# Head of a fused attention and MLP kernel: two raw weight loads behind the stores, sums of squares accumulated on ScalarE, three weight pairs by 16-bit instructions, four filling groups for six

## The chip, the cores and the metric

The kernel runs on one core of one Trainium2 chip. The metric is device time in microseconds (us), the median of several runs. The engines are TensorE (PE in the profile; PEld are its weight loads), VectorE (DVE), ScalarE (ACT), GpSimd (POOL) and SyncE (SP, which issues all transfers of this kernel). Sixteen DMA engines move the data.

## The reference

Three stages follow each other on 2176 tokens of width 512 (4 batches, 8 heads of width 64):

```python
# attention: 32 global tokens see everything; 512 local tokens see the global ones and a band of +-32
s_ll = np.where(np.abs(pos[:, None] - pos[None, :]) <= 32, scale * q_l @ k_l.T, -1e9)
out_l = softmax([scale * q_l @ k_g.T, s_ll]) @ [v_g, v_l]
out_g = softmax(scale * q_g @ [k_g, k_l].T) @ [v_g, v_l]
x = [out_g, out_l] as (B * S, H * D)
# first MLP
xn = x / np.sqrt(np.mean(x * x, axis=-1, keepdims=True) + 1e-06) * rms_g
x = (silu(xn @ w_gate) * (xn @ w_val)) @ w_out          # 512 -> 1536 -> 512
# second MLP
r = np.maximum(x @ w_in, 0.0)
return (s * (r * r) + b) @ w_out2                       # 512 -> 2048 -> 512
```

All inputs are float32.

## The kernel before

**Groups.** The tokens are worked on in five groups of at most 512. The first group is the 512 local tokens of batch 0. For each group come the first MLP (12 slices of its inner width) and the second MLP (16 slices). Between the matmuls of a group, the attention of the next group's tokens is strewn in small steps.

**Weights.** The weights come as 34 pairs of blocks, in the order in which PE uses them. Each block is 512 x 128, and each product is made of three matmuls (L691 to L693) with a high and a low part of both operands: 24 matmuls a pair. A pair arrives as raw 64-bit numbers (1 MB, `load_raw`, tile `wr`, four buffers). `conv_begin` takes the raw numbers apart: ScalarE multiplies the upper 32-bit word into tile `cv` (L192), VectorE makes the missing bits in tile `ce`, clamps `cv` (L205) and joins both (L206). The missing bits are made in one of two ways: with `halves`, two 16-bit instructions on VectorE (L197, L199); without, a copy on ScalarE (L202) and one VectorE instruction (L203). `conv_end` casts the high part on ScalarE (L213), takes the low part on VectorE (L214), loads the next raw pair, and stores the finished pair to device memory (tile `wsc`, 1 MB, L217). Only the first group converts; the others load the stored pairs.

**The head** (`start`). Before the first matmul with weights, the attention of batch 0 must be done, in four units of two heads. Unit u goes through `S_` (scores on PE, then on VectorE the mask, the maximum and the difference, L313 to L315, called a score block in this document, then the exponential on ScalarE, L320), `T_` (transposes on PE, L623, two copies on ScalarE, L624) and `V_` (values on PE, L329, then the shares on VectorE, L336 to L338, then the squares on ScalarE, L634 or L637). `first_norm` makes the inverse root from the sums of squares, scales the four column blocks of the tokens (L538, L540), transposes them on PE (L547) and writes the high and low parts of x (L552, L553). `fill` issues matmuls whose results are not used (L600); one stands ahead of the transposes of `first_norm`.

**Order.** PE's order in the head is written out by `in_turn`, the order of ScalarE, VectorE and SP by `in_line`, which puts each instruction of a list behind the one before it. Pairs 0 and 1 are converted inside the head with `halves`; pair 2 is begun there without `halves` and ended behind the first Silu (`ending`). Behind that, `conv` converts pair n + 4 when PE is through with pair n, and a scheduler fills in the order that the lists leave open. The engines take their instructions strictly in order. SP issues a transfer when the eighth one before it has landed and the buffer is free.

## Time and profile before

| | |
|---|---|
| median of 3 runs | 931.55 us (931.52 to 933.0) |
| the profiled execution | 932.3 us, its span 930.5 us |
| PE busy | 910.2 us, 98% of the span |
| ScalarE, VectorE busy | 389.5 us (42%), 435.4 us (47%) |
| mean granted TensorE clock | 0.989 |
| moved by DMA | 255.77 MB, mean 275 GB/s |
| first matmul of the main part | 43.62 us from the start of the span |

The span runs from the first to the last instruction. A share of busy time is a mean over the head, the first group (in which all weights are converted) and the four others. What a change in one stage is worth is read in that stage.

### The profile page before, as it was taken

How to read it: one execution, taken by the hardware profiler on the slowest of the kernel's cores; microseconds unless marked ns; L12 is line 12 of the kernel's file. 1: busy time of each engine (PE TensorE's matmuls, PEld its weight loads, DVE VectorE, ACT ScalarE, POOL GpSimd, SP SyncE). 2: the span in 40 equal slices, each digit the busy share in tenths (PEclk: the TensorE clock that was granted, in tenths of full speed). 3: DMA queues.
4: the chain of work that ended last, by engine and by line, in shares of the span. 5: the costliest groups of instructions: out<-in, count | busy, mean ns of one | idle time of the engine just before them, and what ended most of it. 6: DMA issues, size and time to landing. Idle time of an engine off the chain costs nothing.

```text
span 930.5 us, 16330 instructions
## 1 busy us (share of the span) xinstructions
PE 910.2 (98%) x6946; PEld 776.0 (83%) x6946; DVE 435.4 (47%) x754; ACT 389.5 (42%) x558; POOL 0.6 (0%) x7
## 2 busy tenths in 40 slices
PE   9799999999999989999999999999999999999998
PEld 6477887877887868888878868888899999999998
DVE  5898889979642232343242232344222244321333
ACT  2787997969433132233223132232233133211322
POOL 0000000000000000000000000000000000000000
PEclk7899999999999999999999999999999999999999
DMA  9999999997976664755566654654588887798780
GB/s 365 392 379 425 368 425 423 395 347 293 372 262 229 246 259 142 276 188 181 205 229 242 241 205 141 211 185 177 197 317 299 287 282 269 281 341 306 286 300 29
DMA packets 43960, 255.77 MB, mean 275 GB/s; under 512 B 5104, under 2 KB 9456, under 8 KB 15984
## 3 DMA queue, kind: packets, MB, share of 16 engines
q1 hardware_dynamic: 43888, 254.73, 73.1%
q8 instruction: 55, 0.90, 0.4%
q14 instruction: 17, 0.14, 0.0%
HBM read 214.60 MB, written 40.11 MB: 274 GB/s over the span
## 4 chain that ended last, share of the span: by engine, by line
PE 94%; ACT 2%; DVE 1%; issue 1%; DMA 1%; SPq 0%; ACTq 0%
PE m L691 16%; PE m L692 16%; PE m L693 16%; PE acc L692 12%; PE acc L691 12%; PE acc L693 12%; PE at L329 2%; PE at L289 1%; PE acc L600 1%; PE at L324 1%; PE at L374 1%; PE at L406 1%; DMA s_k<-in_k_dram 1%; PE at L486 1%; PE m L623 1%
## 5 line engine op out<-in xcount | busy, mean ns | idle before, releaser
L692 PE MATMUL acc<-h,wt 128*128 128x512 f32 (+1 forms) x536 | 193.2, 360 | 0.6 <-DVE h L799 0.3
L693 PE MATMUL acc<-h,wt 128*128 128x512 f32 (+1 forms) x536 | 192.1, 358 | 0.0
L691 PE MATMUL acc<-h,wt 128*128 128x512 f32 (+1 forms) x536 | 185.2, 362 | 0.4 <-ACT h L153 0.4
L691 PE MATMUL m<-x,wt 128*128 128x512 f32 (+1 forms) x480 | 173.0, 361 | 1.9 <-ACT sg L766 1.9
L692 PE MATMUL m<-x,wt 128*128 128x512 f32 (+1 forms) x480 | 172.3, 359 | 0.0
L693 PE MATMUL m<-x,wt 128*128 128x512 f32 (+1 forms) x480 | 172.2, 359 | 0.0
L776 DVE TENSOR_TENSOR a<-sg,m 128x512 f32<-128x512 f32 (+1 forms) x60 | 36.4, 607 | 174.5 <-PE m L693 166.2
L691 PE MATMUL m<-y,wt 128*128 128x512 f32 (+1 forms) x320 | 115.2, 360 | 2.8 <-DVE t L796 2.8
L692 PE MATMUL m<-y,wt 128*128 128x512 f32 (+1 forms) x320 | 115.4, 361 | 0.3 <-DVE y L728 0.3
L693 PE MATMUL m<-y,wt 128*128 128x512 f32 (+1 forms) x320 | 114.8, 359 | 0.0
L796 DVE SCALAR_TENSOR_TENSOR t<-m,ct,r 128x512 f32<-128x512 f32 (+1 forms) x80 | 53.6, 670 | 129.7 <-ACT r L795 129.3
L692 PEld LDWEIGHTS acc<-h,wt 128*128 128x128 f32 x536 | 100.6, 188 | 14.4 <-DVE h L799 1.9
L691 PEld LDWEIGHTS acc<-h,wt 128*128 128x128 f32 x536 | 100.4, 188 | 14.4 <-ACT h L153 0.8
L693 PEld LDWEIGHTS acc<-h,wt 128*128 128x128 f32 x536 | 100.7, 188 | 12.5 <-issue 0.2
L795 ACT ACTIVATE r<-m 128x512 f32<-128x512 f32 (+1 forms) x80 | 42.4, 533 | 156.5 <-PE m L693 156.1
L691 PEld LDWEIGHTS m<-x,wt 128*128 128x128 f32 x480 | 90.0, 188 | 14.7 <-ACT sg L766 2.8
L692 PEld LDWEIGHTS m<-x,wt 128*128 128x128 f32 x480 | 90.1, 188 | 11.5 <-DVE x L553 0.2
L693 PEld LDWEIGHTS m<-x,wt 128*128 128x128 f32 x480 | 90.1, 188 | 11.3
L766 ACT ACTIVATE sg<-m 128x512 f32<-128x512 f32 (+1 forms) x60 | 32.0, 534 | 129.3 <-PE m L693 129.2
L799 DVE SCALAR_TENSOR_TENSOR h<-t,ct,h 128x512 fp32r<-128x512 f32 (+1 forms) x79 | 53.1, 672 | 40.2 <-ACT h L798 36.8
L798 ACT ACTIVATE h<-t,ct 128x512 fp32r<-128x512 f32 (+1 forms) x79 | 52.3, 662 | 44.7 <-DVE t L796 39.9
L691 PEld LDWEIGHTS m<-y,wt 128*128 128x128 f32 x320 | 60.4, 189 | 11.0 <-DVE t L796 3.3
(158 smaller groups left out, 953.3 us busy)
## 6 DMA issues: line engine op xcount, KB each, us to landing
wt<-wsc SPq DMA_DIRECT2D x136, 1024.0 KB, 4.9
wr<-in_w_dram SPq DMA_DIRECT2D x34, 1024.0 KB, 9.1
wsc<-wt SPq DMA_DIRECT2D x34, 1024.0 KB, 8.6
vr<-in_v_dram SPq DMA_DIRECT2D x12, 1105.0 KB, 8.5
fk<-in_k_dram SPq DMA_DIRECT2D x12, 784.0 KB, 6.2
fq<-in_q_dram SPq DMA_DIRECT2D x12, 272.0 KB, 7.8
out_dram<-z SPq DMA_DIRECT2D x12, 256.0 KB, 4.2
s_v<-in_v_dram SPq DMA_DIRECT2D x2, 1040.0 KB, 8.9
```

Source lines behind the costliest of these rows:

```text
L289: mms.append(PE.matmul(bk[32 * g:32 * g + 32, h, 128 * c:128 * c + 128].rearrange("p (a n) -> p a n", a=2), lhsT=qr[x, SG + 32 * i:SG + 32 ...
L324: in_turn([PE.transpose(flat[:, 128 * a:128 * a + 128], pp[:, a], ident) for a in range(8)])
L329: return [PE.matmul(bk[32 * g:32 * g + 32, h, 65 * c:65 * c + 65], lhsT=t(4 * h + c, g), rhs=vr(4 * c + g)[:, 65 * h:65 * h + 65]) for c i ...
L691: mms = [PE.matmul(out_, lhsT=wh, rhs=xh, start=first, stop=False), PE.matmul(out_, lhsT=wh, rhs=xl, start=False, stop=False), PE.matmul(o ...
L692: PE.matmul(out_, lhsT=wh, rhs=xl, start=False, stop=False),
L693: PE.matmul(out_, lhsT=wl, rhs=xh, start=False, stop=last)]
L766: recent["A"] = A.activation(out=sg[:, :N], in_=gb[:, :N], func=AF.Silu)
L776: V.tensor_tensor(out=a[:, :N], in0=sg[:, :N], in1=vb[:, :N], op=ALU.mult)
L795: A.activation(out=r[:, :N], in_=hb[:, :N], func=AF.Relu)
L796: V.scalar_tensor_tensor(out=t[:, :N], in0=hb[:, :N], scalar=ct[:, C_S:C_S + 1], in1=r[:, :N], op0=ALU.mult, op1=ALU.mult)
L798: recent["A"] = A.activation(out=h[:, 0, :N], in_=t[:, :N], func=AF.Identity, bias=ct[:, C_B:C_B + 1])
L799: recent["V"] = V.scalar_tensor_tensor(out=h[:, 1, :N], in0=t[:, :N], scalar=ct[:, C_B:C_B + 1], in1=h[:, 0, :N].bitcast(F32), op0=ALU.add ...
```

## The change

The first batch of raw loads is three instead of four; the first of them is issued ahead of the second unit's values, the second ahead of the fourth's. The fourth raw load stands behind the store of pair 0 on SP's queue, the fifth behind the store of pair 1, and the loads of the first attention units, which stood behind the fourth raw load, stand behind the fifth. The sums of squares of units 2 and 3 are accumulated on ScalarE in four instructions each, as those of units 0 and 1 were; before, one instruction squared the whole and VectorE summed. The fourth column block is scaled on VectorE. Pair 2 is converted with `halves`, wholly behind the first Silu, and one more raw load is issued behind it. The filling ahead of the norm's transposes has four matmuls for six. The lists of ScalarE and VectorE in the head are written anew. The first attention step of the first group is let off 12 us after the group's start by the planner's count, not 10.

```diff
@@ conv_end @@
-        nc.sync.dma_start(out=wsc[n], in_=wn.bitcast(F32))
+        stores[n] = nc.sync.dma_start(out=wsc[n], in_=wn.bitcast(F32))
@@ load_qk @@
-                in_line([raws[3], d])
+                in_line([raws[4], d])
@@ first_norm @@
-            if c == 3:
-                scaled.append(A.mul(out=o, in_=o, mul=r[:, c:c + 1]))
-            else:
-                scaled.append(V.tensor_scalar(out=o, in0=o, scalar1=r[:, c:c + 1], scalar2=None, op0=ALU.mult))
+            scaled.append(V.tensor_scalar(out=o, in0=o, scalar1=r[:, c:c + 1], scalar2=None, op0=ALU.mult))
@@ start @@
         ld_qk(3)
+        load_raw()
         ld_v(1)
         ld_v(2)
         load_raw()
         ld_v(3)
-        for _ in range(3):
-            load_raw()
+        load_raw()
...
-            if u < 2:
-                sq[u] = [A.activation(out=j[:, c], in_=uu[:, c], func=AF.Square, accum_out=ss[:, c, u:u + 1])
-                         for c in range(4)]
-            else:
-                sq[u] = A.activation(out=j, in_=uu, func=AF.Square)
-                rd[u] = V.tensor_reduce(out=ss[:, :, u], in_=j, axis=mybir.AxisListType.X, op=ALU.add)
+            sq[u] = [A.activation(out=j[:, c], in_=uu[:, c], func=AF.Square, accum_out=ss[:, c, u:u + 1])
+                     for c in range(4)]
...
-            roots, r, scaled, xa, xd = first_norm(sm, lambda b: fill(b, 6))
+            roots, r, scaled, xa, xd = first_norm(sm, lambda b: fill(b, 4))
...
-        g2, a2, d2 = conv_begin(2)
-        in_line([ex[0], ex[1]] + cp[0] + [ex[2]] + cp[1] + [ex[3]] + cp[2] + sq[0] + [a0[0]] + cp[3] + sq[1]
-                + [a1[0], a0e, sq[2], a2[0], sq[3], a1e] + roots + [scaled[3]] + xa + [a2[1]])
-        in_line([am[0], am[1], am[2], am[3], ev[0], d0[0], d0[1], d0[2], d0[3], ev[1], d1[0], d1[1], ev[2], d1[2], d1[3], ev[3],
-                 rd[2], rd[3], sums, r[0], r[1]] + scaled[:3] + [d0e] + xd + [d1e, d2[0], d2[1], d2[2]])
-        begun.append(d2[2])
-        ending.append(lambda: conv_end(2, g2))
+        in_line([stores[0], raws[3]])
+        in_line([stores[1], raws[4]])
+        in_line([ex[0], ex[1], a0[0]] + cp[0] + [ex[2]] + cp[1] + [a1[0], ex[3]] + cp[2] + [a0e] + sq[0] + cp[3]
+                + sq[1] + sq[2] + sq[3] + roots + xa + [a1e])
+        in_line([am[0], am[1], d0[0], d0[1], am[2], d0[2], am[3], d0[3], ev[0], d1[0], d0e, ev[1], d1[1], ev[2], ev[3],
+                 d1[2], sums, r[0], r[1]] + scaled + [d1[3]] + xd + [d1e])
+        begun.append(d1e)
+
+        def third_pair(sg):
+            g2, a2, d2 = conv_begin(2, True)
+            in_line([a1e, sg, a2[0]])
+            in_line([d1e, d2[0], d2[1], d2[2], d2[3]])
+            conv_end(2, g2)
+            load_raw()
+
+        ending.append(third_pair)
@@ main loop @@
-            sched["ok"] = sched["t"] + (0.0 if gi else 10.0)
+            sched["ok"] = sched["t"] + (0.0 if gi else 12.0)
...
-                in_line([recent["A"], ending.pop(0)()[0]])
+                ending.pop(0)(recent["A"])
                 conv(C_LEAD - 1)
```

The order on three queues, first before, then of the change. SP's queue in the head, from its 11th transfer on (`wr` are raw loads, `s_v`, `s_w` and `s_r` values of the units 1 to 3, `wsc0` and `wsc1` the stores of pairs 0 and 1, `fq` and `fk` the loads of the first attention units):

```order
L576 DMA s_v_112<-in_v_dram 128x2080
L576 DMA s_w_116<-in_v_dram 128x1950
L576 DMA s_r_115<-in_v_dram 128x130
L171 DMA wr_132<-in_w_dram 128x1024
L576 DMA s_w_117<-in_v_dram 128x1950
L576 DMA s_r_115<-in_v_dram 128x130
L171 DMA wr_136<-in_w_dram 128x1024
L171 DMA wr_138<-in_w_dram 128x1024
L171 DMA wr_140<-in_w_dram 128x1024
L265 DMA fq_744<-in_q_dram 128x544
L265 DMA fk_745<-in_k_dram 128x1568
```

Of the change:

```order
L171 DMA wr_129<-in_w_dram 128x1024
L573 DMA s_v_112<-in_v_dram 128x2080
L573 DMA s_w_116<-in_v_dram 128x1950
L573 DMA s_r_115<-in_v_dram 128x130
L171 DMA wr_134<-in_w_dram 128x1024
L573 DMA s_w_117<-in_v_dram 128x1950
L573 DMA s_r_115<-in_v_dram 128x130
L171 DMA wr_138<-in_w_dram 128x1024
L217 DMA wsc0_625<-wt_620 128x2048
L171 DMA wr_623<-in_w_dram 128x1024
L217 DMA wsc1_639<-wt_634 128x2048
L171 DMA wr_637<-in_w_dram 128x1024
```

The first raw load moved from place 14 to 11, the second from 17 to 15, the third stands where it stood, and behind it nothing is issued before the store of pair 0.

VectorE in the head, from the third score block on (`s_p_150` and `s_p_148` are its results, `ce_613` and `cv_614` belong to pair 0, `ce_627` to pair 1):

```order
L313 TENSOR_TENSOR acc1_248<-acc1_248,ct_102 128x16x32
L314 TENSOR_REDUCE mx_290<-acc1_248 128x8
L315 TENSOR_TENSOR s_p_150<-acc1_248,mx_290 128x1024
L313 TENSOR_TENSOR acc0_308<-acc0_308,ct_102 128x16x32
L314 TENSOR_REDUCE mx_349<-acc0_308 128x8
L315 TENSOR_TENSOR pm0_105<-acc0_308,mx_349 128x1024
L336 TENSOR_SCALAR rs_400<-at_367 128x8
L337 RECIPROCAL rs_400<-rs_400 128x8
L338 TENSOR_TENSOR u_152<-at_367,rs_400 128x2x4x64
L197 TENSOR_SCALAR ce_613<-wr_132 128x1024
L199 TENSOR_SCALAR ce_613<-wr_132 128x1024
L205 TENSOR_SCALAR cv_614<-cv_614 128x1024
```

Of the change:

```order
L197 TENSOR_SCALAR ce_613<-wr_129 128x1024
L199 TENSOR_SCALAR ce_613<-wr_129 128x1024
L313 TENSOR_TENSOR acc1_246<-acc1_246,ct_102 128x16x32
L314 TENSOR_REDUCE mx_288<-acc1_246 128x8
L315 TENSOR_TENSOR s_p_148<-acc1_246,mx_288 128x1024
L205 TENSOR_SCALAR cv_614<-cv_614 128x1024
L313 TENSOR_TENSOR acc0_306<-acc0_306,ct_102 128x16x32
L314 TENSOR_REDUCE mx_347<-acc0_306 128x8
L315 TENSOR_TENSOR pm0_105<-acc0_306,mx_347 128x1024
L206 SCALAR_TENSOR_TENSOR cv_614<-cv_614,ce_613 128x1024
L336 TENSOR_SCALAR rs_398<-at_365 128x8
L337 RECIPROCAL rs_398<-rs_398 128x8
```

The conversion of pair 0 moved from behind the first shares to between the second and the fourth score block.

VectorE late in the first group, in the second MLP (`at_2153` and `at_2155` are the values of an attention unit that PE computes in a burst, `m_2258` and `m_2260` the product of one inner slice; L796, in the change L798, frees that bank):

```order
L336 TENSOR_SCALAR rs_2210<-at_2153 128x8
L206 SCALAR_TENSOR_TENSOR cv_2275<-cv_2275,ce_2274 128x1024
L337 RECIPROCAL rs_2210<-rs_2210 128x8
L338 TENSOR_TENSOR u_1262<-at_2153,rs_2210 128x2x4x64
L414 TENSOR_SCALAR rg_2214<-at_2153 128x1
L796 SCALAR_TENSOR_TENSOR t_2289<-m_2258,ct_102,r_2288 128x512
L415 RECIPROCAL rg_2214<-rg_2214 128x1
L214 TENSOR_TENSOR wt_2281<-cv_2275,wt_2281 128x2x512
L416 TENSOR_SCALAR og_1451<-at_2153,rg_2214 128x64
L796 SCALAR_TENSOR_TENSOR t_2337<-m_2307,ct_102,r_2336 128x512
```

Of the change, without the five rows ahead (L336, L337, L338, L203, L414), up to the next L798:

```order
L798 SCALAR_TENSOR_TENSOR t_2291<-m_2260,ct_102,r_2290 128x512
L205 TENSOR_SCALAR cv_2228<-cv_2228 128x1024
L415 RECIPROCAL rg_2216<-rg_2216 128x1
L206 SCALAR_TENSOR_TENSOR cv_2228<-cv_2228,ce_2227 128x1024
L416 TENSOR_SCALAR og_1462<-at_2155,rg_2216 128x64
L203 TENSOR_SCALAR ce_2276<-ce_2276 128x1024
L205 TENSOR_SCALAR cv_2277<-cv_2277 128x1024
L206 SCALAR_TENSOR_TENSOR cv_2277<-cv_2277,ce_2276 128x1024
L801 SCALAR_TENSOR_TENSOR h2_2292<-t_2291,ct_102,h2_2292 128x512
L214 TENSOR_TENSOR wt_2234<-cv_2228,wt_2234 128x2x512
L798 SCALAR_TENSOR_TENSOR t_2339<-m_2309,ct_102,r_2338 128x512
```

Nine instructions, six of them of conversions, stand between the two, where there were three. On PE the burst of values moved too: before, it stood three matmuls ahead of the end of `m_2307`, whose successor needs the bank of `m_2258`; now 22 matmuls (12 of an output slice, 10 of `m_2309`) stand between the burst and the successor.

## Rows read from the trace of the kernel before

**Rows 1.** The page, part 4: the chain that ended last, shares of the span.
```profile
PE 94%; ACT 2%; DVE 1%; issue 1%; DMA 1%; SPq 0%; ACTq 0%
```
**Rows 2.** Waits of PE, whole kernel: us in total, times, longest.
```profile
PE m L691 <- DVE t L796: 2.8, 2, 2.1
```
**Rows 3.** Timeline of PE, 26 to 44: start, us, what, count, idle before.
```profile
27.32 0.30 PE L329 MATMUL acc<-s_v,ptf 128*32 128x65 f32 x3 [2.61 <-issue]
...
33.50 0.27 PE L329 MATMUL at<-s_w,ptf 128*32 128x65 f32 x1 [3.00 <-issue]
...
34.08 8.03 PE L600 MATMUL acc<-ones 128*128 128x512 f32 x12
...
40.23 1.02 PE L600 MATMUL acc<-ones 128*128 128x512 f32 x2
...
41.95 1.91 PE L547 MATMUL acc<-ct,u 128*128 128x128 f32 x16
...
43.62 0.71 PE L691 MATMUL m<-x,wt 128*128 128x512 f32 x2
```
**Rows 4.** Instruction queue: whole kernel, 31.0:31.5, 280.4:280.5 (packets, MB, share); engines at 280.
```profile
q8 instruction: 55, 0.90, 0.4%
...
q8 instruction: 1, 0.02, 13.3%
...
q8 instruction: 1, 0.02, 72.1%
...
280.00:281.00 1.00, 1.00 (x6) 0.47 (x6) 0.23 (x1) 0.73 (x2) 0.00 (x0) 1.00 0.45 172
```
**Rows 5.** SP's 11th transfer: its issue, and its time from issue to landing.
```profile
6.60 0.33 SPq L576 DMA_DIRECT2D s_v<-in_v_dram  x1
...
s_v<-in_v_dram SPq DMA_DIRECT2D x1, 1040.0 KB, 9.8
```
**Rows 6.** Timeline of VectorE, 16 to 43.
```profile
16.57 0.70 DVE L313 TENSOR_TENSOR acc<-acc,ct 128x512 f32<-128x512 f32 x1 [2.10 <-PE acc L305]
...
18.56 1.23 DVE L315 TENSOR_TENSOR s_p<-acc,mx 128x1024 f32<-128x1024 f32 x1
...
24.85 0.74 DVE L197 TENSOR_SCALAR ce<-wr 128x1024 int16<-128x1024 int16 x1
...
35.39 0.16 DVE L336 TENSOR_SCALAR rs<-at 128x8 f32<-128x8 f32 x1
...
36.43 0.68 DVE L638 TENSOR_REDUCE ss<-s_j 128x4 f32<-128x512 f32 x1
...
38.03 0.17 DVE L657 TENSOR_REDUCE ss<-ss 128x4 f32<-128x16 f32 x1
...
39.45 1.28 DVE L540 TENSOR_SCALAR u<-u,r 128x512 f32<-128x512 f32 x3
```
**Rows 7.** Timeline of ScalarE, 25 to 50.
```profile
25.84 0.32 ACT L634 ACTIVATE s_j<-u 128x128 f32<-128x128 f32 x1
...
27.02 1.13 ACT L192 ACTIVATE cv<-wr 128x1024 f32<-128x1024 f32 x1
...
28.31 1.07 ACT L624 COPY ptf<-m 128x512 f32<-128x512 f32 x2 [0.17 <-PE m L623]
...
33.39 1.03 ACT L213 CAST wt<-cv 128x1024 fp32r<-128x1024 f32 x1
...
49.46 1.89 ACT L202 COPY ce<-wr 128x2048 int16<-128x2048 int16 x1
```
**Rows 8.** VectorE at 207; engines, 210 to 220 (sums, PEclk, DMA share, GB/s).
```profile
207.08 0.17 DVE L336 TENSOR_SCALAR rs<-at 128x8 f32<-128x8 f32 x1 [1.52 <-PE at L406]
...
210.00:220.00 10.00, 10.00 (x37) 8.14 (x38) 8.34 (x14) 9.97 (x15) 0.00 (x0) 0.83 0.99 388
```
**Rows 9.** Engines in two stretches of the first group (PE, PEld, DVE, ACT, POOL, PEclk, DMA).
```profile
60.00:70.00 10.00, 10.00 (x104) 8.00 (x103) 9.95 (x13) 10.00 (x10) 0.00 (x0) 1.00 1.01 421
...
230.00:240.00 10.00, 10.00 (x46) 8.29 (x45) 8.71 (x16) 5.24 (x9) 0.00 (x0) 1.00 0.61 216
```

More of the change, by code (lines that the diff above doesn't have):

```diff
@@ L141, in attn_moe_kernel @@
     wt, wraw, wsc, left = {}, {}, {}, {}
-    raws = {}
+    raws, stores = {}, {}
     nraw = [0]
```

## The prediction, made before the kernel ran

> **What bounds the kernel now.** I read the chain that ended last first: TensorE (PE) holds 94% of it [rows 1]. So time can only be won where PE waits, or where it does work that is not part of the result. I then read PE's waits over the whole kernel and its timeline in the first 45 us. PE reaches the first matmul of the main part (L691) at 43.62 us, and from there on it hardly waits. The largest later wait for one engine is 2.8 us in two pieces, for VectorE's L796 [rows 2]. The head is different: two waits, 2.61 and 3.00 us, end in "issue", which means that nothing in the profile ends them [rows 3]. Then 12 fill records run from 34.08, and the transposes of the first norm start only when the fill is over, at 41.95.
>
> What are the two "issue" waits? They break off in the middle of a run of equal matmuls, so no data can be missing. I looked at the DMA view in slices: the queue of kind "instruction" moves 55 packets, 0.90 MB in the whole kernel, some 16 KB each, and in the head one is moved from 31.0 on, inside the second wait [rows 4]. I read them as PE's program, loaded late because data transfers have the DMA engines full. A later stretch shows what an emptying queue does: the packet at 280.4 is moved in the very microsecond in which the transfers run out (DMA share 0.45) [rows 4].
>
> **The head, step by step** (times on the axis of the profile before). *First raw load.* It becomes the 11th load. The 11th is issued at 6.60 and lands 9.8 later, at 16.4 [rows 5]. It is as large as the s_v load that it displaces, and the transfers land in order at about 0.42 MB per us [rows 9], so I keep 16.4. Behind it come s_v, s_w, the second raw load, s_w and the third: the second lands near 23.9, the third near 29.0.
>
> *VectorE.* Two 16-bit instructions (0.63 each, from L197's 0.74 less the overlap [rows 6]) now stand ahead of the third score block. They start at 16.4, so the block starts at 17.7 and not at 16.57. It takes 3.2 (L313, L314, L315: 0.70, 1.23, 1.23 [rows 6]) and ends at 20.9. L205 0.6, the fourth block, L206 1.1: 25.7. The first shares take 1.04 (from 35.39 to 36.43 [rows 6]): 26.8, then L197: 27.4.
>
> *ScalarE.* The multiply of pair 0 (1.13 [rows 7]) fits before the first copies. The two copies of the second unit's transposes end at 22.9; then the queue stands until the second raw load at 23.9. The multiply ends at 25.0, the last exponential (about 1.05) at 26.0, two copies (0.95, from 1.07 [rows 7]) at 26.9, the cast of pair 0 (1.03 [rows 7]) at 27.9, four squares (1.18, from 25.84 to 27.02 [rows 7]) at 29.0, the last two copies at 30.1.
>
> *VectorE again.* The low part of pair 0 waits for the cast: 28.0 to 29.1; shares 30.2; L199 30.8; shares 31.9. From then on the last shares may run. Today they start at 35.39 [rows 6], although PE has been done with their values since 34.1: VectorE is behind.
>
> *TensorE.* The first code wait stays, since the queue is as full as before: 27.3. The last values need the copies of 30.1 and come to the code boundary at 30.9. Today the code comes at 33.5. After the change the loads end at 29.0; the store of pair 0 is issued only when VectorE has the low part, 29.1, and its first bytes come later still (no row prices that, and I count nothing for it). So there is a hole in the transfers when the packet wants to go. I take it as moved at about 29.2 rather than 31.0, and the wait as over 2.5 later (as 31.0 to 33.5 [rows 3, 4]), near 31.7. The bounds are 30.9 (no wait) and 33.5 (all of it stays). I take the value near the first, by the packet at 280.4.
>
> *The norm.* The last values end 0.6 behind the code (33.50 to 34.08 [rows 3]), at 32.2. Last shares to 33.3, four squares to 34.5 (both sums on VectorE, 0.68 each [rows 6], are gone; today the second ends just before L657 at 38.03). From L657 to the first scaling there are 1.42 (38.03 to 39.45 [rows 6]): 36.0. Four scalings at 0.40 (1.28 for three [rows 6]; the fourth was on ScalarE, beside them) end at 37.6. Four fills are eight records, 0.43 each at full clock (from 40.23 to 41.95 the last four of twelve [rows 3]): 32.2 + 3.4 = 35.6, so the fill no longer holds the transposes. The last four transposes of a bank cannot start before 37.6; 13 or so of 16 remain at 0.104 (1.67 for 16 [rows 3]). First main matmul: **39.0 instead of 43.62, 4.6 less.**
>
> If the code wait stays whole, the values end at 34.1 as today. The first eight of the twelve fill records end where the ninth starts, 40.23 [rows 3]; scaling is done by 39.8. Transposes at 40.23 and not 41.95: **1.7 less**, all of it from the two fills.
>
> The Trainium skill speaks against my reading of the waits: "Runtime: NRT & Kernel Launch", Instruction fetch mechanics, says that engines fetch code in 16 KiB blocks and that crossing a boundary is "mostly hidden". The trace agrees on the size and not on the rest (2.61 and 3.00 us open); with code always hidden, the head would end at 39.0 or a little before, whatever the loads do, since VectorE is the last to be ready.
>
> **After the head** (times from the first main matmul). *Pair 1* costs nothing: its cast comes behind the four x copies, its low part behind the four low parts of x, ready at 3.6, and PE needs it after 24 matmuls at 0.23 [rows 9], 5.5. *The loads behind its store* are all issued from 3.6 on: store, two raw loads, both pairs of attention loads, 1.05 + 2.1 + 2.2 MB at 0.42 with some 2 of startup: the raw load of pair 4 lands near 11, the attention loads from 16 to 19. ScalarE asks for the one at 11.7, PE for the others after two more pairs and a half, near 21. Tight, and hidden by the work of pairs 0 to 3; if it were late, ScalarE would stand ahead of the cast of pair 3.
>
> *Third pair.* Its multiply now comes behind the first Silu, its cast behind two multiplies (1.13), a 1.89 copy [rows 7], two short casts and the second Silu: about 6.3 after the Silu ends, at 12. PE gets there after 48 matmuls at 0.23 (46 records touch ten microseconds, about 44 start in them [rows 9]), 11.0. PE waits up to 1.1; part of that wait exists today, and I charge **+0.5**.
>
> *The wait at 208.* VectorE stood 1.52 for PE's values at L336, with L796 queued behind it; PE then waited 2.1 of the 2.8 for that L796 [rows 2, 8], and its clock, 0.83 over the next 10 us [rows 8], fell to the lower level for 3.4 us of them: 1.7 more. In the new order PE has 22 matmuls, 5.0 us, between those values and the block that needs this L796, and VectorE needs 2.6 for the queue. I take back 3.8. But the next L796 now has nine instructions between it and the first, six of them of conversions: it comes about 9.5 us behind the values, against 10.5 us of cover on PE (22 and 24 matmuls), and each of the six can itself wait for ScalarE: a wait of 0 to 4 there, four being the price of the old wait. I charge 2.0. Net **-1.8**.
>
> *From the second stage on* the order is the same on every engine, so the waits there stay.
>
> *The sum:* -4.6 + 0.5 - 1.8 = -5.9. The profiled run took 932.3 for a span of 930.5; the median of the runs is 931.55, and I subtract from that: 925.6. The allowance of 2.0 could as well be 2.5, so I say **926**.
>
> **Rivals.** *The code wait stays* (the packet is late for another reason than the full queue): -1.7 + 0.5 - 1.8 = -3.0, **928.5**. For it: nothing in the trace names who waits for that packet. Against: 280.4. Chance 0.28.
>
> *The transfers that are not made in the head are missing later: slower.* At the time at which today two more raw loads, both pairs of attention loads and a value load have landed, nothing of these is: 2.1 + 2.2 + 1.1 MB, 5.4 MB, 12.8 us at the rate above. In the first stage the DMA engines are full (1.01 from 60 to 70 [rows 9]), so the debt is paid back slowly, and on ScalarE each conversion's first copy stands ahead of a Silu or a cast that PE needs. Four raw buffers let a load start three conversions ahead, at one pair of 24 matmuls 16.5 us; a landing takes some 9.8 of them [rows 5], which leaves 6.7. Beyond these ScalarE waits 12.8 - 6.7 = 6.1. The sign turns when PE feels more than 4.1 of them with the wait at 208 as it is: -4.6 + 0.5 + 6.1 = +2.0, **933.5**, and up to 940 with all 12.8. Against: a pair is converted well before PE needs it, so ScalarE's wait need not reach PE. Chance 0.12.
>
> *The raw load is late.* L197 and the multiply of pair 0 stand ahead of the score blocks; VectorE has no slack after 16.4, so each microsecond by which the load misses 16.4 moves the head's end by one. If the two large loads that it overtakes went first all the same, 2 MB at the rate above, 4.8 would be lost and the head would win nothing: **930 to 932**. Chance 0.1.
>
> *The forecast*: 0.5, with a range of its own of 922 to 929.
>
> **Range and chances.** A difference under 0.2%, 1.9 us, is no change here. Forecast: nearly all of it faster. First rival: two thirds faster, the rest no change. Second: mostly slower or no change. Third: no change, with a third faster. Faster 0.70, same 0.18, slower 0.12. The range goes from the best end of the forecast, 922, to 932.5, which leaves out the bad end of the second rival.
>
> **What would show it.** Right: the first main matmul near 39; one code wait of about 2.6 and a second under 1; no DMA traffic around 29.5 to 31; transposes that start on VectorE's scaling and not on the fill; no wait at L336's place near 200. Wrong: a second code wait of 3, the first score blocks on VectorE later than 18, ScalarE standing on raw loads between 60 and 120 us, or the clock at half after the transposes, since PE now stands about 2 us between fill and transposes: this would cost 1.7 for each 3.4 us at the lower level, and would bring the forecast to the first rival's time.

## The result

The changed kernel is slower by 1.3%: 943.44 us median of 5 runs (942.17 to 944.01), against 931.55 (927.69 to 933.16) of the kernel before on the same chip, a ratio of 1.0128 (95% interval 1.0111 to 1.0146). I had predicted 926, and faster with a chance of 0.70. The profiled execution has a span of 942.2 us (before: 930.5).

**The head came out as predicted.** PE's timeline (start, us, what, count, idle before), against [rows 3]:

```profile
27.30 0.30 PE L329 MATMUL acc<-s_v,ptf 128*32 128x65 f32 x3 [2.25 <-issue]
...
30.03 0.32 PE L329 MATMUL at<-s_w,ptf 128*32 128x65 f32 x8 [0.35 <-ACT ptf L621]
...
32.47 3.67 PE L597 MATMUL acc<-ones 128*128 128x512 f32 x8 [0.66 <-DVE rs L336]
36.86 2.83 PE L544 MATMUL acc<-ct,u 128*128 128x128 f32 x16 [0.72 <-DVE u L537]
39.44 0.71 PE L693 MATMUL m<-x,wt 128*128 128x512 f32 x2
```

A code wait is, here and below, an idle time of PE that ends in "issue", which the prediction reads as a wait for PE's own program. The first one stays and the second is gone; the fill is four matmuls long (eight records), and the transposes (L544) now start on VectorE's scaling (L537). The first main matmul is at 39.44, 4.2 us earlier than in [rows 3]; I had 39.0.

**Behind the head PE waits for weights** (tile `wt`), which it never did before. Its waits, 45 to 260 us (us in total, times, longest):

```profile
PE m L693 <- ACT wt L213: 6.9, 3, 5.4
PE m L695 <- DVE wt L214: 2.7, 3, 1.1
PE acc L693 <- ACT wt L213: 2.2, 2, 1.7
PE acc L694 <- DVE h L801: 1.0, 1, 1.0
PE m L693 <- ACT sg L768: 0.2, 1, 0.2
```

That is 13.0 us. In the same stretch of before PE waited five times, 3.6 us in all, none of it for weights: the line of [rows 2] and these three.

```profile
PE acc L691 <- ACT h L153: 0.4, 1, 0.4
PE m L692 <- DVE y L728: 0.3, 1, 0.3
PE m L691 <- ACT sg L766: 0.2, 1, 0.2
```

The longest wait of the change, 5.43 us, ends at 168.37. The engines in stretches (sums of busy time, then PEclk, DMA share, GB/s) show what came before it and after it:

```profile
25.00:30.00 5.00, 2.42 (x77) 1.96 (x74) 4.30 (x9) 5.00 (x15) 0.00 (x0) 1.00 0.48 190
30.00:35.00 5.00, 4.15 (x70) 2.38 (x71) 3.92 (x10) 4.19 (x25) 0.00 (x0) 1.00 0.95 310
35.00:40.00 5.00, 4.08 (x22) 2.34 (x20) 4.40 (x12) 3.58 (x7) 0.00 (x0) 1.00 0.28 115
40.00:45.00 5.00, 5.00 (x23) 3.99 (x22) 4.34 (x6) 1.99 (x4) 0.00 (x0) 1.00 0.25 105
45.00:160.00 115.00, 111.18 (x891) 87.18 (x891) 95.76 (x131) 89.32 (x89) 0.00 (x0) 1.00 1.01 415
160.00:170.00 10.00, 4.16 (x15) 2.58 (x14) 6.18 (x10) 9.97 (x11) 0.00 (x0) 0.80 0.85 316
170.00:180.00 10.00, 9.30 (x30) 7.44 (x31) 8.57 (x12) 8.42 (x10) 0.00 (x0) 0.69 0.96 324
```

From 25 to 45 us the DMA engines lack 0.52, 0.05, 0.72 and 0.75 of 5 us each: 10.2 us of transfers that are not made (before, the share was 0.93 to 1.03 there). From 45 to 160 us they are full, as they were before, so there is next to no room to make it up. The row of before:

```profile
45.00:160.00 115.00, 114.08 (x907) 91.18 (x906) 103.06 (x138) 97.25 (x97) 0.00 (x0) 1.00 0.99 400
```

Behind the wait PE's clock is at the lower level for some 10 us (0.80 and 0.69 are means of the two levels, 1.2 and 2.4 GHz).

The sum, by two places that both kernels have: from the first main matmul to the wait at L324 of the second group (343.80 before, 352.26 after) are 300.2 us before and 312.8 after, 12.6 more. Waits are 13.0 - 3.6 = 9.4 of them, the clock the rest. With the head's -4.2 that makes +8.5. The other 3.2 of the two spans lie behind, where the order is the same, and come from two drops of the clock (see the end). The second place, before and after:

```profile
343.80 1.09 PE L324 MATMUL at<-ct,pm 128*128 128x128 f32 x8 [2.06 <-ACT pg L385]
...
352.26 1.09 PE L324 MATMUL at<-ct,pm 128*128 128x128 f32 x8 [2.06 <-ACT pg L385]
```

This stretch, from the first main matmul to L324, is called the first stretch below; it is read from each kernel's trace.

In the chain that ended last PE has 85% (94% in [rows 1]), and transfers 6%:

```profile
PE 85%; DMA 6%; ACT 4%; DVE 4%; issue 1%; SPq 0%; ACTq 0%; DVEq 0%
```

This share does not make transfers the cause: two kernels below that are as slow (945.64 and 945.11 us) have 1% and 2% of them in their chains.

### The profile page after: what moved, and what is told of

It is laid out like the page before. It is cut to its first block, busy times and chain, and to the rows that moved or that the text cites. A ratio compares the mean times of both kernels' runs of the same rounds, so it can differ in the third digit from the quotient of the medians.

```text
span 942.2 us, 16339 instructions
## 1 busy us (share of the span) xinstructions
PE 913.4 (97%) x6942; PEld 776.9 (82%) x6942; DVE 436.5 (46%) x754; ACT 389.1 (41%) x570; POOL 0.6 (0%) x7
## 4 chain that ended last, share of the span: by engine, by line
PE 85%; DMA 6%; ACT 4%; DVE 4%; issue 1%; SPq 0%; ACTq 0%; DVEq 0%
PE m L695 15%; PE m L693 15%; PE m L694 15%; PE acc L693 11%; PE acc L694 11%; PE acc L695 11%; DMA fq<-in_q_dram 2%; DMA vr<-in_v_dram 2%; DMA wr<-in_w_dram 2%; PE at L329 1%; PE at L324 1%; PE at L289 1%; ACT ce L202 1%; PE at L374 1%; PE at L406 1%
## 5 line engine op out<-in xcount | busy, mean ns | idle before, releaser
L694 PEld LDWEIGHTS acc<-h,wt 128*128 128x128 f32 x536 | 100.7, 188 | 15.7 <-DVE h L801 3.3
L798 DVE SCALAR_TENSOR_TENSOR t<-m,ct,r 128x512 f32<-128x512 f32 (+1 forms) x80 | 53.6, 670 | 127.2 <-ACT r L797 127.0
L797 ACT ACTIVATE r<-m 128x512 f32<-128x512 f32 (+1 forms) x80 | 42.6, 532 | 153.3 <-PE m L695 153.0
L801 DVE SCALAR_TENSOR_TENSOR h<-t,ct,h 128x512 fp32r<-128x512 f32 (+1 forms) x79 | 53.1, 672 | 40.9 <-ACT h L800 39.8
```

What stands on the lines that cost most here:

```text
L694: PE.matmul(out_, lhsT=wh, rhs=xl, start=False, stop=False),
L797: A.activation(out=r[:, :N], in_=hb[:, :N], func=AF.Relu)
L798: V.scalar_tensor_tensor(out=t[:, :N], in0=hb[:, :N], scalar=ct[:, C_S:C_S + 1], in1=r[:, :N], op0=ALU.mult, op1=ALU.mult)
L801: recent["V"] = V.scalar_tensor_tensor(out=h[:, 1, :N], in0=t[:, :N], scalar=ct[:, C_B:C_B + 1], in1=h[:, 0, :N].bitcast(F32), op0=ALU.add ...
```

## The experiments

"Before" was timed beside each, 931.5 us each time. A ratio is to it, with its 95% interval. **Theory**, as I held it at first: the transfers not made in the head are missing in the first group, and PE waits for the weights. **Rivals:** the new order on the engines, the planner's 12 us, or the third pair.

### Which part of the change costs

**All loads in front again** (the rest of the change kept):

```diff
         ld_v(3)
         load_raw()
+        load_raw()
...
-        in_line([stores[0], raws[3]])
-        in_line([stores[1], raws[4]])
...
-                in_line([raws[4], d])
+                in_line([raws[3], d])
```

> The changed kernel with its loads as early as before: the fourth raw load and the loads of the first two attention units stand in the head's batch again, nothing is tied to a store; squares, halves, fills, lists and the planner's 12 us stay. Theory (the transfers that are not made in the head are missing from 45 to 160 us): the waits of PE for converted weights around 140 to 170 us (9.6 us in 6) shrink under 2 us, the first main matmul goes back to about 41.9 because the second code wait returns (2 to 3 us), and the time is 927 to 931. Rival (the new order of ScalarE and VectorE, the third pair or the planner's offset makes the conversions late): the waits for weights stay over 6 us and the time is 938 to 946.

Measured: 930.48 us, 0.9988 (0.9973 to 1.0003). The waits for weights go, but for one of 1.7 us; a code wait of 1.8 us is back in place of the second, and the first main matmul is at 41.18. So the loads' move, with the order that comes of it, costs all of the loss, and of the head's gain 1.7 us hangs on it.

**The loads' move alone**, put into the kernel before (batch of three, both ties, one more raw load behind pair 2):

```diff
-        for _ in range(3):
+        for _ in range(2):
             load_raw()
...
+        in_line([stores[0], raws[3]])
+        in_line([stores[1], raws[4]])
```

> The kernel before with one part of the change alone: three raw loads in the head's batch, the fourth behind the store of pair 0 and the fifth behind the store of pair 1, the first attention loads behind the fifth. The store of pair 0 stands late in this order (its low part is taken behind the scalings), so the DMA engines would be empty from about 29 to 41 us, some 5 MB. Theory (missing transfers): no second code wait, but the head ends at 42 or later since VectorE's sums are still there; waits of PE for converted weights appear between 85 and 175 us, 8 to 14 us in all, and the time is 938 to 948. Rival (the new order on the engines, not the loads): 929 to 933.

945.64 us, 1.0149 (1.0118 to 1.0181): the loss without the rest of the change. Its head ends at 41.50, behind VectorE's scalings, and the transfers pause from 28 to 40 us.

**One tie instead of two**:

```diff
-        in_line([stores[1], raws[4]])
```

> The changed kernel without one of its two ties: the fifth raw load and the attention loads no longer wait for the store of pair 1; only the fourth raw load stands behind the store of pair 0. The DMA share of 0.0 to 0.2 from 37 to 43.4 us should become 1. Theory (missing transfers): the first main matmul stays near 39.4 without a second code wait, about 7 us of transfers (3 MB of 4.4) are made in the hole, the waits for weights around 140 to 170 us fall from 9.6 us to under 4, and the time is 926 to 933. Rival (order of the engines): waits and time stay, 940 to 946. If the second code wait comes back, the head ends near 41 and the time is 2 us more.

932.61 us, 1.0009 (0.9996 to 1.0022). The head ends at 39.80, the pause is some 3 us (share 0.38 from 28 to 32), and of PE's waits for weights one of 0.3 us is left. A wait of 3.0 us for VectorE's `t` (L797) at 160 to 163 takes back most of the head's gain.

**The planner's start at 10 us again**:

```diff
-            sched["ok"] = sched["t"] + (0.0 if gi else 12.0)
+            sched["ok"] = sched["t"] + (0.0 if gi else 10.0)
```

> The changed kernel with the planner's first attention step at 10 us as before, not 12. Theory (missing transfers): the waits for weights stay within 3 us of 9.6 and the time is 939 to 947. Rival (the planner's offset jams the conversions with the attention steps around 160 us): the waits go under 3 us and the time is 927 to 932.

945.15 us, 1.0131 (1.0096 to 1.0165). Not the planner, though the longest wait is now 7.5 us for `t`, so it moves where PE stands.

### How much the missing transfers cost

**More transfers in the kernel before**, read by nobody, four and then two of 1 MB:

```diff
+        for i in range(4):
+            spare = dr_p.tile([128, 2, 512], I64, name=f"spare{i}")
+            extra.append(nc.sync.dma_start(out=spare, in_=w[i]))
+        in_line([stores[1]] + extra)
```

> The kernel before with four transfers of 1 MB more (raw weights copied to a spare place in device memory, read by nobody), put behind the store of pair 1 and ahead of the raw load of pair 6, so that the transfers after the head are 4.2 MB more, about 10 us at 0.42 MB per us, as many as the changed kernel left unmade in its head; the head itself is that of before. Theory (in the first group the transfers are the bound, and what is missing or added is paid nearly in full): the last raw load is issued 7 to 10 us later than the 214.3 of before, PE waits for converted weights between 80 and 180 us, and the time is 938 to 946. Rival of the forecast (four raw buffers absorb 6.7 us of it): 932 to 936. Rival (only the place of the two loads matters): 930 to 933.

> The same with two such transfers, 2.1 MB, 5 us. Theory, paid in full: 935 to 938; with a slack of 2 to 3 us in the conversions: 933 to 935. Rival of the forecast (6.7 us are absorbed): 930.5 to 932.5.

940.69 us, 1.0091 (1.0065 to 1.0117), and 938.06, 1.0063 (1.0039 to 1.0087). More transfers cost time, as the theory has it, but not in proportion: 5 us of them cost 6.5 and 10 us only 9.1 (in the first stretch 7.7 and 8.9, as the head ended earlier). With two, PE waits 4.7 us for `t` and not for weights. The scheduler had written another order for each, so the size is not to be read from these two.

**Fewer transfers in the changed kernel** (it leaves out the attention of two units):

```diff
+        if i in (1, 3):
+            raw_u[i] = [raw_u[i - 1][0], raw_u[i - 1][1], None]
+            return
...
+        if i in (1, 3):
+            raw_u[i][2] = raw_u[i - 1][2]
+            return
```

> The changed kernel with fewer transfers in the first group: of the first four attention units every second one reads the loads of the unit ahead of it (so the attention of these two units is left out and another stands in its place), 4.4 MB less, about as many as its head left unmade; the loads stay tied to the stores. Theory (amount of transfers): the waits for converted weights between 140 and 175 us fall from 9.6 us under 3, the last raw load is issued near 214 and not 223, and the time is 925 to 931, since the head's 4.2 us are kept. Rival (the late place of the two raw loads, or the order of the engines): 938 to 945.

936.47 us, 1.0047 (1.0031 to 1.0063): 7 of the 12 us come back, less than I expected; a wait of 4.3 us for `t` at 166 remains.

**The fourth raw load tied to the last exponential**:

```diff
+            if n == 3:
+                G.tensor_copy(out=wraw[n].bitcast(F32)[:, 0, 0:1], in_=last_p[0][:, 0, 0:1])
```

> The changed kernel without both ties; the fourth raw load waits instead for the last exponential of the head (GpSimd writes one element of its buffer behind it), so that the hole in the transfers is only some 1 to 2 us long, near 27 to 28.5, and the attention loads follow at once. Theory: the last raw load is issued near 213.5 to 215; if the hole suffices for the code packet, the first main matmul is at 39.4 to 40.5 and the time 927.5 to 930.5; if not, the second code wait is back, the first main matmul is near 41.7 and the time 930 to 932, as with the loads in front.

935.41 us, 1.0041 (1.0027 to 1.0054), slower than both cases allowed. The tie left no pause at all (share 1.01 to 1.03 from 24 to 44 us), a code wait of 1.3 us is back, the head ends at 41.57. With every transfer made in time it still lost 3.9 us, in spite of a head that is 2.0 shorter: the first stretch took 302.9 against 300.2, with a wait of 3.0 for `t` at 164, and 3.2 more lie behind L324. So there is a cost that is not a missing transfer.

### The jam at 160 us

At the start of the first group's second stage ScalarE loads a table and makes two exponentials (3.3 us), and in some orders a conversion's cast, its copy and another exponential stand behind them, ahead of the Relu for which VectorE and PE wait. I put the first Relu and `t` ahead of the newest conversion, in the run with one tie:

```diff
+            if gi == 0 and f == 0:
+                in_line([ra, latest_conv[0]])
+                in_line([ta, latest_conv[1]])
```

> The changed kernel without the tie to the store of pair 1 (as in the run with one tie) and with one order more: at the start of the first group's second stage the first Relu and the first squared product come ahead of the latest conversion on ScalarE and VectorE. Theory (what the run with one tie still lost is a jam on ScalarE and VectorE at 156 to 163 us, where a conversion stood ahead of the piece that PE waited 3.0 us for): that wait goes under 1 us, the clock does not fall behind it, and the time is 926.5 to 930, faster than the kernel before. Rival (the 3 us of transfers that the hole still costs are what is paid; the wait moves to another place): 931 to 934.

934.40 us, 1.0028 (1.0018 to 1.0039): a miss. The wait fell from 3.0 to 1.0 us, and three of 1.6 to 1.7 for weights came up, at 235.5, 243.9 and 251.2 us. Mending one place moved the wait to another.

**The exponentials behind a cast**, in the changed kernel:

```diff
+            if i == 2:
+                in_line([casts[-1], r[0]])
```

> The changed kernel with both ties, and with the two exponentials of the second attention pair put behind the latest cast of a conversion on ScalarE, so that the 3.2 us of table load and exponentials at 160 to 163.4 us do not stand ahead of the cast for which PE waited 5.4 us. Theory (the late transfers used up the converted pairs in stock, and the jam on ScalarE at 160 us then reached PE; both take part): the wait of 5.4 us shrinks to 1 to 3, the smaller waits for weights (0.5 to 1.1 us) stay, the last raw load stays near 220, and the time is 936 to 941. Rival A (the jam alone is the loss): 928 to 932. Rival B (the transfers alone are the loss, the waits move on): 942 to 945.

941.29 us, 1.0102 (1.0088 to 1.0116), just above the range of the theory: the wait of 5.4 becomes 2.2 and the small ones stay, as the theory had it; the jam is worth about 2 of the 12 us.

**Tie to the cast of pair 0**, with the Relu first and no tie to a store:

```diff
+            if n == 3:
+                G.tensor_copy(out=wraw[n].bitcast(F32)[:, 0, 0:1], in_=wt[0][:, 0, 0, 0:1].bitcast(F32))
```

> As the first run of this call, but the fourth raw load waits for the cast of pair 0 (GpSimd writes one element behind it), not for the issue of the store, so that its transfer can start some 1 to 2 us earlier. Theory: the hole in the transfers shrinks from some 3 us to 1 to 2, the second code wait stays under 1 us, the first main matmul is near 40, and the time is 926 to 929.5. If the hole is gone, the second code wait is back (1.3 to 3 us), the first main matmul near 41.5, and the time 929 to 932.

931.39 us, 0.9998 (0.9989 to 1.0007). The pause is short (share 0.76 from 28 to 32), the second code wait 0.55 us, and the head ends at 39.67, all as hoped; the time is not (926 to 929.5 was expected). The first stretch took 300.8, and 2.8 us of the gain are lost behind L324.

### Is the last raw load the pace?

In all kernels up to here the time from the issue of the last raw load to L324 in the second group was 125 to 130 us, so I took that load for the pace. The loads of units 4 and 5, which only the second group needs, were put behind it:

```diff
-                load_v(i + 2)
-                load_v(i + 3)
+                if i != 2:
+                    load_v(i + 2)
+                    load_v(i + 3)
...
+        elif i in (4, 5):
+            in_line([raws[PAIRS - 1], d])
...
+        if gi == 0 and ph == 2 and f == 10:
+            for i in (4, 5):
+                load_qk(i)
+                load_v(i)
```

(and the same for `load_qk`), in four kernels: the changed one, the one before, the one with all loads in front, and the one with the tie to the cast.

> The changed kernel with both ties, and with the loads of the fifth and sixth attention units (4.3 MB, which only the second group needs) behind the last raw load, not at 140 to 163 and 212 us. Theory (the last raw load sets the pace of the first group: from its issue to PE's L324 in the second group it is 126 to 130 us in all kernels so far): 4.3 MB, 10 us of transfers, leave the stretch ahead of it, but only from 140 us on, so the wait of 5.4 us near 168 shrinks and does not vanish; the last raw load is issued at 213 to 218 and not at 223.2, and the time is 932 to 938. Rival (the converted pairs were short already at 140 us and stay so): 940 to 944.

> The kernel before with that same move of 4.3 MB of loads behind the last raw load, and nothing else. Theory (the transfers pace the first group before the change too, so a head that ends earlier could bring little): the last raw load is issued at 205 to 209 and not at 214.3, and the time is 925 to 929. Rival (PE paces it, the transfers have slack): 930 to 932.

> The changed kernel with its loads as early as before (nothing tied to a store) and the loads of the fifth and sixth unit behind the last raw load. Theory: the head ends near 41.5, the transfers no longer hold the first group, and the time is 922 to 927, faster than both kernels. Rival (the first group is held by PE and by the jam at 160 us): 929 to 931.

> As the run in which the fourth raw load waits for the cast of pair 0 (931.4), with the loads of the fifth and sixth unit behind the last raw load. Theory: the head ends near 39.7, without the second code wait, the transfers no longer hold the first group, and the time is 920 to 926. Rival (held by PE and the jam): 929 to 931.5.

Measured: 939.88 (1.0089, 1.0070 to 1.0108), 931.60 (0.9997, 0.9983 to 1.0011), 931.36 (1.0007, 0.9993 to 1.0020) and 928.35 (0.9968, 0.9955 to 0.9981). Of the expectations only the rival of the second, 930 to 932, held. The idea fell with the second: in the kernel before, the DMA share at 160 to 180 us went from 1.0 to 0.8, and the last raw load was still issued at 214.17 (214.31). From 160 us on, raw loads wait for buffers, and so for PE; the constant distance was a consequence, not a cause. The fourth kernel is faster than both, by 0.3% of before.

### Transfers or order?

Each kernel with other loads had also got another order of conversions from the scheduler. The last three kernels keep an order: the sequence of another kernel's instructions on PE, ScalarE and VectorE is written out and imposed, and only the transfers differ. No run has a written-out order with its own transfers, so what the writing out costs by itself is not measured.

```diff
+    for e, turns in TURNS.items():
+        in_line([told[e][a + i] for a, n in turns for i in range(n)])
```

**Early loads, order of the changed kernel:**

> The loads of the run with all loads in front (930.5), and on TensorE, ScalarE and VectorE the order of the changed kernel, instruction for instruction: the order is written out, so that only the transfers differ from the changed kernel. Theory A (it is the late transfers themselves that PE waits for): the stock of converted pairs at 140 us is 2 or more, the waits for weights there go, and the time is 929 to 934. Theory B (the transfers count only through the order that the scheduler wrote for them, with each conversion put late): the stock at 140 us is under 1, the wait of 5.4 us at 168 stays above 3, and the time is 938 to 944, with the head at 41.

945.11 us, 1.0144 (1.0130 to 1.0159). All waits of the changed kernel return, with all loads early and a DMA share of 0.95 where the changed kernel had 1.01:

```profile
45.00:160.00 115.00, 111.68 (x894) 87.44 (x892) 95.70 (x131) 87.18 (x87) 0.00 (x0) 1.00 0.95 369
```

The first stretch took 312.0 us, 11.8 of the 12.6 that the changed kernel lost there. Of its PE timeline and that of the changed kernel, 140 to 175 us, the rows with a wait (in the written-out kernels every instruction has the line of one helper):

```profile
143.86 0.73 PE L182 MATMUL m<-x,wt 128*128 128x512 f32 x2 [0.58 <-ACT wt L182]
147.47 2.57 PE L182 MATMUL m<-x,wt 128*128 128x512 f32 x10 [1.04 <-DVE wt L182]
158.56 1.19 PE L182 MATMUL m<-y,wt 128*128 128x512 f32 x4 [0.86 <-ACT wt L182]
...
170.53 1.22 PE L182 MATMUL m<-y,wt 128*128 128x512 f32 x2 [5.43 <-ACT wt L182]
```

```profile
141.71 0.50 PE L693 MATMUL m<-x,wt 128*128 128x512 f32 x1 [0.58 <-ACT wt L213]
145.31 0.50 PE L695 MATMUL m<-x,wt 128*128 128x512 f32 x1 [1.04 <-DVE wt L214]
156.40 0.50 PE L693 MATMUL m<-y,wt 128*128 128x512 f32 x1 [0.86 <-ACT wt L213]
...
168.37 0.80 PE L693 MATMUL m<-y,wt 128*128 128x512 f32 x1 [5.43 <-ACT wt L213]
```

The waits agree to the hundredth, 2.2 us later because the head ends 2.4 later. So in the changed kernel PE waits for casts that stand late in ScalarE's order, not for a transfer that is on its way. Its own trace says the same: from 45 to 175 us no wait of PE, ScalarE or VectorE in it ends with a transfer.

**Late loads, order of the run with all loads in front:**

> The other crossing: the changed kernel with its loads tied to the stores, and on TensorE, ScalarE and VectorE the order of the run with all loads in front, written out. Theory A: the conversions stand on raw loads that are not there, ScalarE holds up Silu and casts behind them, and the time is 938 to 950, with waits of 10 us or more on PE from 60 to 170 us. Theory B: 928 to 933, since the order is that of the fast variant and the head ends at 39.5.

939.62 us, 1.0081 (1.0067 to 1.0096). Of the waits for weights one of 1.7 us is left; a wait of 10.3 us for `a` ends at 58.8 instead, and the first stretch took 310.4. VectorE's timeline at that place:

```profile
53.90 0.36 DVE L181 COPY qf<-fq 64x32 f32<-64x32 f32 x2 [10.78 <-DMA fq<-in_q_dram]
56.45 0.36 DVE L181 COPY qf<-fq 64x32 f32<-64x32 f32 x2 [2.19 <-DMA fq<-in_q_dram]
56.83 1.37 DVE L181 TENSOR_SCALAR ce<-wr 128x1024 int16<-128x1024 int16 x2
58.08 0.68 DVE L181 TENSOR_TENSOR a<-sg,m 128x512 f32<-128x512 f32 x1
```

VectorE stands 13.0 us in two pieces on the attention loads, which are issued at 44.95 and 46.74, behind the store of pair 1 at 43.14, and the `a` that PE needs is queued behind.

**More transfers, order of the kernel before** (4.2 MB on another queue):

```diff
+        for i in range(4):
+            spare = dr_p.tile([128, 2, 2, 512], F32, name=f"spare{i}")
+            nc.gpsimd.dma_start(out=spare, in_=wsc[1])
```

> The kernel before, its order on TensorE, ScalarE and VectorE written out and so kept to the instruction, with 4 transfers of 1 MB more behind the store of pair 1 on another queue (issued by GpSimd, the stored pair 1 copied to a place that nobody reads): 4.2 MB, 10 us of the transfers' time near 48 to 70 us. Theory A, paid in full: 937 to 944. With the stock of converted pairs that the kernel before has at 140 us (3 pairs) to draw on: 932 to 936, as PE does not wait until the stock is gone. Theory B (the order decides): 930.5 to 932.5.

939.27 us, 1.0080 (1.0066 to 1.0094). With the order unchanged, 10 us more of transfers cost 7.7 (7.8 in the first stretch). PE waits for `h` and for `pg`, 2.3 us each, and work that these need is queued behind a load: on ScalarE, which stands 5.0 us on a raw load, and on VectorE, which stands 4.0 on an attention load. ScalarE's timeline at the first place:

```profile
75.43 1.90 ACT L179 COPY ce<-wr 128x2048 int16<-128x2048 int16 x1 [5.03 <-DMA wr<-in_w_dram]
80.15 1.90 ACT L179 COPY ce<-wr 128x2048 int16<-128x2048 int16 x1 [0.82 <-DMA wr<-in_w_dram]
81.95 0.61 ACT L179 CAST h<-a 128x512 fp32r<-128x512 f32 x1
```

The cast of `h` stands behind both waits in ScalarE's queue. PE did not wait for weights here.

The two crossings in one table (us):

| | order of the run with all loads in front | order of the changed kernel |
|---|---|---|
| early loads | 930.48 | 945.11 |
| late loads | 939.62 | 943.44 |

## Why the prediction was wrong

**Right, step by step:** the first raw load lands at 16.7 (16.4 said); the score block starts at 18.03 (17.7); the cast-bound low part of pair 0 ends at 29.6 (29.1); the store is issued at 29.62, with a hole in the transfers; the second code wait is gone, so my rival "the code wait stays" did not come; the sums are made from 34.9 (34.5), the scalings at 38.0 (37.6), the first main matmul is at 39.44 (39.0). The third pair made no new wait (0.23 us behind the first Silu, as before). No wait stands at the old place at 208. Two new ones, at 232.6 and 248.2, are 2.7 us together, near the 2.0 that I allowed; but that is luck, since they are for `h` and for a cast, and my 2.0 was for the next `t` (L798).

**The step that failed** is the part on what comes after the head. It charged +0.5 for the third pair and -1.8 for the wait at 208, -1.3 in all; the first stretch measured +12.6. For the conversions between the third pair and 208 it charged nothing, and the reason stands against the second rival: "a pair is converted well before PE needs it, so ScalarE's wait need not reach PE". Both halves of that sentence were wrong, and the price beside it was too low.

*"A pair is converted well before PE needs it"* was not read from the trace. It can be: casts of pairs (ScalarE, tile `wt`) and main matmuls, 24 to a pair, up to 140 us. The columns of these windows are PE, PEld, VectorE, ScalarE; of before, after, and the run with all loads in front, in this order:

```profile
0.00:140.00 140.00, 88.28 (x376) 69.83 (x377) 21.90 (x18) 18.95 (x19) 0.94 0.98 392
```

```profile
0.00:140.00 140.00, 91.20 (x384) 70.86 (x384) 19.50 (x16) 16.79 (x16) 0.96 0.93 374
```

```profile
0.00:140.00 140.00, 90.63 (x385) 71.46 (x386) 22.91 (x19) 20.06 (x19) 0.98 0.99 398
```

Before: 19 casts against 376/24 = 15.7 pairs used, 3.3 in stock. After: 16 against 16.0, none. With all loads in front: 3.0. The same up to 100 us, before and after:

```profile
0.00:100.00 100.00, 52.10 (x222) 41.11 (x223) 12.19 (x10) 10.46 (x10) 0.91 0.98 392
```

```profile
0.00:100.00 100.00, 55.65 (x235) 43.40 (x236) 12.16 (x10) 11.55 (x11) 0.95 0.89 353
```

There the changed kernel still had 1.2 pairs in stock, and before 0.7. So the head did not use up a stock; from 100 to 140 us, while PE used some 6 pairs in both, 5 casts were made where before had made 9, and the stock was never built. Then each delay on ScalarE (the table and exponentials at 160) was PE's.

*"ScalarE's wait need not reach PE"*: it reaches PE without any shortage of weights. With the order of before kept and 4.2 MB added, the stock at 140 us was 3.5 pairs (18 casts, 349 matmuls), and the time still rose by 7.7 us, since `h` and `pg` stood behind the waits for loads.

*The price.* I let four raw buffers absorb 6.7 of 12.8 us. With the order kept, 10 us of added transfers cost 7.7 us, so little over 2 were absorbed.

*The second rival was not right either.* It has 12.8 us at most, and 12.6 were measured, but this is luck: the rival has ScalarE standing on raw loads, and no wait of ScalarE in the changed kernel from 45 to 175 us ends with a transfer.

*What neither the rival nor I had seen:* the loss does not need the transfers to be late when the kernel runs. Moving the loads in the source was enough for another order of conversions (all loads in front differs from the changed kernel in nothing else), and that order alone gave 945.1 with early loads, 11.8 of the 12.6 us. Late loads with the better order gave 939.6, so they cost by themselves, too, but by another wait (VectorE on attention loads). The two are not to be added: the order was written around late loads and holds their cost. That the scheduler counts on a later arrival is argued from this, not shown; why its order makes few casts from 100 to 140 us stays open.

The half clock behind the wait of 5.4 us, which I had named as a danger only behind the transposes, took some 3 us more than before's drop behind the wait at 208.

One reading of the prediction was wrong without harm: the largest later wait of PE for one engine was not the 2.8 us for `t` but 3.2 in two pieces for `pg` at L324, and that one is the same after the change.

**The head's gain** may be partly luck of the profile I read. The three kernels with before's head and added transfers (which came behind the head) ended it at 40.7 to 40.9, with a second code wait of 1.5 us, where before had 43.62 and 3.00; a fourth, with a change far behind the head, had 43.86 and 3.00. One execution is not enough to price a wait that varies.

## What to carry

Before a forecast charges nothing for a stretch, count there products made against products used, and compare each engine's whole queue, not only its ends: the order between 45 and 200 us of the changed kernel was the loss. Where a scheduler writes the order, a moved load rewrites every engine's queue; write one kernel's order out and cross it with the other's transfers to tell which of the two costs. With the DMA engines at 0.99 or more for a hundred microseconds, 10 us of added transfers cost 7.7 with the order kept, and a stock of converted pairs did not pay for them, because other work stood behind the waits for loads. The kernel with a pause of about 1 us in the head and two units' loads moved behind the last raw load was the only one faster than both, 928.35; its order was written anew too, so how much is due to the moves is not shown.

## What was not expected of the hardware

- **The second code wait of PE follows the transfers.** With the share at 1.0 it was 1.3 to 3.0 us in all kernels; with a pause of some 3 us or more just ahead it was absent, with about 1 us 0.55 and 0.94. The first code wait does not go by the share alone: with 1.0 or more from 24 to 28 us it was 1.5 to 3.2 us in nine kernels, but 0.18 with all loads in front and units 4 and 5 late, and absent with early loads in the order of the changed kernel. The Trainium skill, "Runtime: NRT & Kernel Launch", Instruction fetch mechanics, has the crossing of a 16 KiB boundary as "mostly hidden"; at the second crossing these runs agree only where the transfers pause.
- **Equal waits, unequal clocks.** At L324 in the second group PE stands 2.06 and then 0.82 us, before and after alike. Before, the clock stays full in the 12 us from there; after, it falls to the lower level for a few microseconds, and a second time later on, where before stayed full (1.00 from 554 to 562):

```profile
354.00:358.00 4.00, 3.83 (x11) 3.08 (x12) 1.38 (x2) 1.53 (x3) 0.00 (x0) 0.61 0.92 388
...
566.00:570.00 4.00, 4.00 (x14) 3.17 (x13) 0.69 (x1) 0.66 (x2) 0.00 (x0) 0.66 0.20 74
```

  The clock is 0.39 and 0.34 short of full over 4 us each, which is 1.6 and 1.4 us of PE's time, most of the 3.2 that the change lost behind L324. The spans behind L324 range from 586.7 to 589.9 over all profiled kernels. What decides it stays open.
